# One decode step of attention and a gated feed-forward layer on one core: the V loads change their issuing engine

## The chip, the cores and the metric

The program runs on one core of one Trainium2 chip. The metric is the device time of one execution in microseconds (us); the number given for a kernel is the median of its runs. A profiled execution has its own time, and its trace covers a span that is a little shorter.

## What is computed

One token passes a pre-norm attention block whose keys and values lie in a cache, and then a feed-forward block with a ReLU gate. All is float32: 32 heads of 192 numbers each, 8192 cached positions, a model width of 640, and 1536 in the feed-forward block.

```python
h  = x + A(layernorm(x), k_cache, v_cache, wq, wo)
h2 = h + B(layernorm(h), W_gate, W_up, W_down)

def A(x, k_cache, v_cache, wq, wo):
    q = (x @ wq) as (B, H, 1, Dh)
    scores = einsum("bhqd,bhkd->bhqk", q, k_cache) * Dh ** -0.5
    o = einsum("bhqk,bhkd->bhqd", softmax(scores), v_cache)
    return o as (B, 1, H * Dh) @ wo

def B(x, W_gate, W_up, W_down):
    gate, up = x @ W_gate, x @ W_up
    return (where(gate > 0, gate, 0) * up) @ W_down
```

The caches are by far the largest inputs: 32 heads with 6.29 MB of K and 6.29 MB of V each, 403 MB of the 446 MB that are read.

## The kernel before

The 8192 positions of a head lie as 64 positions on each of 128 partitions, so one head's K, or its V, is one tile of 128 x 12288 numbers, loaded by one DMA of 128 rows of 49,152 bytes. All these tiles come from the pool `kv`, which has three places of that size and no more; the three loads of `wq` at the start and the feed-forward weights `ffn_a` and `ffn_b` at the end use the same three places. A load into a place waits until the readers of the tile that was there have finished.

In what follows K(h) and V(h) are the tiles of head h. Per head the work is this.

- **K to scores.** VectorE multiplies K by the query in four pieces (line 183), GpSimd adds the upper half of each product to the lower (line 184), and VectorE sums what is left in four pieces (line 188). After the last of these K's place is free.
- **Softmax.** The generator `softmax_steps` is run between the pieces of the next head's line 183: maximum over a partition (193), a transpose on TensorE (195), maximum over all (198), a broadcast on TensorE (200), the scaled maximum and the exponential on ScalarE (202, 205), the sum over partitions on TensorE (207) and its reciprocal on VectorE (210). So the softmax of head h lies in head h+1's scores.
- **Values.** 32 matmuls on TensorE (line 225, which the profile counts as 64) read all of V(h) and the weights `p`; after the last of them V's place is free. ScalarE then scales the result into `ob` (line 228).
- **Output.** `finish_steps` transposes `ob` on TensorE and VectorE (240, 244), also between the pieces of a later head, and once per group of four heads (two groups of two at the end) multiplies by that group's part of `wo` (254), 1.97 MB for four heads, loaded into a pool of its own with two places.

The query of a head (line 169) is a small matmul into one of two PSUM buffers.

The main loop asks in iteration h for K(h+1), then for V(h), then does the scores of head h+1 and the values of head h. All loads of the loop are issued by SP, on its one DMA queue, in the order K(1), V(0), K(2), V(1) and so on; only the two tiny loads of `x` are issued by ScalarE. A wait in front of a load holds up everything behind it on the issuing engine. A Tile scheduler turns the program into one instruction stream per engine and decides which of the three places each tile gets. The calls marked `keep` hold VectorE's order as written; the rest may be moved.

After the loop the tail loads `W_up` and part of `W_gate` into `ffn_a`, the rest of `W_gate` and `W_down` into `ffn_b`, 11.8 MB in all, each when a place is free (lines 294 to 298), and does the feed-forward block while the weights arrive.

Of the kernel before, what the change touches and what calls it, by code (L numbers as in the profile page):

```python
# [14 lines left out]
def kernel(  # L15
# [12 lines left out]
    nc = tc.nc  # L28
# [9 lines left out]
    TW = R * DH  # L38
# [11 lines left out]
    kf, vf = kc[0], vc[0]  # L50
# [20 lines left out]
    for j in range(0, DJ, 2):  # L71
        n = min(2, DJ - j)
# [1 line left out]
        nc.sync.dma_start(t3, wq_v[:, j:j + n, :])  # L74
        wq_ts += [t3[:, i, :] for i in range(n)]

    def load_kv(src, h, parts):
        t = kv.tile([P, 2 * TW], F32, name="kv_t")
        v = src[h].rearrange("(p r) d -> p (r d)", p=P)
        b = 0  # L80
        for n in parts:
            nc.sync.dma_start(t[:, b:b + n], v[:, b:b + n])  # L82
            b += n
        return t

    def load_wo(gi):
        hs = GROUPS[gi]
        j = len(hs) * DH // P
        t = wts.tile([P, j, D], F32, tag="wo_t", name="wo_t")
        r0 = hs[0] * DH  # L90
        nc.sync.dma_start(t, wo[r0:r0 + len(hs) * DH, :].rearrange("(p j) n -> p j n", p=P))
        return t
# [73 lines left out]
    def query(h):  # L166
        g, i = divmod(h, HPQ)
        q = ps_q.tile([P, QB], F32, tag="q", name="q")
        nc.tensor.matmul(q[:, 0:DH], sel[:, g, :], q4[:, i * DH:(i + 1) * DH], start=True, stop=True)  # L169
        return q[:, 0:DH]  # L170
# [5 lines left out]
    def head_step(q, kt, *works):  # L176


        sc = small.tile([P, NS], F32, name="sc")
        k3 = kt.rearrange("p (r d) -> p r d", d=DH)  # L180
        parts = [(i0, k3[:, i0:i0 + SUB, :]) for i0 in range(0, NS, SUB)]
        for i0, ks in parts:
            keep(nc.vector.tensor_mul(ks, ks, q[:, None, :].to_broadcast([P, SUB, DH])))  # L183
            nc.gpsimd.tensor_add(ks[:, :, 0:HD], ks[:, :, 0:HD], ks[:, :, HD:DH])  # L184
            for w in works:
                next(w, None)
        for i0, ks in parts:
            keep(nc.vector.reduce_sum(sc[:, i0:i0 + SUB], ks[:, :, 0:HD], axis=AX.X))  # L188
        return sc

    def softmax_steps(sc, res):
        mp = small.tile([P, 1], F32, name="mp")
        keep(nc.vector.reduce_max(mp, sc, axis=AX.X))  # L193
        pt = ps_s.tile([P, 512], F32, name="ps_small")
        keep(nc.tensor.transpose(pt[0:1, 0:P], mp, ident))  # L195
        yield
        m1 = small.tile([1, 1], F32, name="m1")
        keep(nc.vector.reduce_max(m1, pt[0:1, 0:P], axis=AX.X))  # L198
        pb = ps_s.tile([P, 512], F32, name="ps_small")
        nc.tensor.matmul(pb[:, 0:1], ones[0:1, :], m1, start=True, stop=True)  # L200
        nb = small.tile([P, 1], F32, name="nb")
        nc.scalar.mul(nb, pb[:, 0:1], -SCALE)  # L202
        p = small.tile([P, NS], F32, name="p")
        rs = small.tile([P, 1], F32, name="rs")
        nc.scalar.activation(p, sc, AF.Exp, bias=nb, scale=SCALE, accum_out=rs)  # L205
        pl = ps_s.tile([P, 512], F32, name="ps_small")
        nc.tensor.matmul(pl[:, 0:1], ones, rs, start=True, stop=True)  # L207
        yield
        rl = small.tile([P, 1], F32, name="rl")
        keep(nc.vector.reciprocal(rl, pl[:, 0:1]))  # L210
        res += [p, rl]
        yield
# [8 lines left out]
    def values_of(h, p, rl, vt):  # L221
        po = pos[h % 2]
        for i in range(NP):
            g = i % NQ
            nc.tensor.matmul(po[g * Q:g * Q + 2, :], p[:, 2 * i:2 * i + 2],  # L225
                             vt[:, 2 * i * DH:(2 * i + 2) * DH], start=(i < NQ), stop=(i >= NP - NQ))
        ob = small.tile([P, 2 * DH], F32, name="ob")
        nc.scalar.activation(ob, po, AF.Copy, scale=rl)  # L228
        return ob

    def finish_steps(h, ob, oT, wo_t):

        gi, i = group_of[h]
        U = NQ // len(GROUPS[gi])
        W = DH // U
        pt = ps_s.tile([P, 512], F32, name="ps_small")
        for u in range(U):
            q0 = (i * U + u) * Q
            for k in range(2):
                nc.tensor.matmul(pt[q0:q0 + Q, 0:W], par[:, k, :], ob[:, k * DH + u * W:k * DH + (u + 1) * W],  # L240
                                 start=(k == 0), stop=(k == 1))
        yield
        s = slice(i * U * Q, (i + 1) * U * Q)
        keep(nc.vector.transpose(oT[s], pt[s, 0:W].rearrange("p (c j) -> p j c", c=Q)))  # L244
        yield
        split = h >= H - 2
        if not split and i < len(GROUPS[gi]) - 1:
            return
        if not split:
            s = slice(0, P)  # L250
        J = wo_t.shape[1]
        for j in range(J):
            for g in range(NQ):
                nc.tensor.matmul(acc[g * Q:(g + 1) * Q, :], oT[s, j, :], wo_t[s, j, g * DG:(g + 1) * DG],  # L254
                                 start=False, stop=(h == H - 1 and j == J - 1))
        yield

    sc = head_step(query(0), load_kv(kf, 0, [2 * TW]))
    done = iter(())
    for h in range(H):  # L260
        gi, i = group_of[h]
        if i == 0:
            wo_t = load_wo(gi)
            oT = small.tile([P, len(GROUPS[gi]) * DH // P, Q], F32, tag="oT", name="oT")
        sm = []
        soft = softmax_steps(sc, sm)
        if h + 1 < H:
            kt = load_kv(kf, h + 1, [2 * TW])
            vt = load_kv(vf, h, [2 * TW])
            sc = head_step(query(h + 1), kt, soft, done)  # L270
        else:
            vt = load_kv(vf, h, [TW] + [TW // 4] * 4)
        for w in (soft, done):
            for _ in w:
                pass
        done = finish_steps(h, values_of(h, *sm, vt), oT, wo_t)
# [99 lines left out]
```

## Time and profile before

| | |
|---|---|
| median of 3 runs | 1045.99 us (1045.82 to 1046.0) |
| the profiled execution | 1045.67 us, of which the trace spans 1043.9 us |
| VectorE busy | 666.0 us, 64% of the span |
| GpSimd busy | 440.1 us, 42% |
| TensorE busy | 409.2 us, 39% |
| ScalarE busy | 45.5 us, 4% |
| read from HBM | 445.91 MB, 427 GB/s over the span |

All traces here are of one core. Times in rows are in us from the start of the span unless marked ns. A row of a timeline has the start, the length, the engine, the line, the operation, output and input, the count, and in brackets the idle time of the engine before it and what ended that. SPq and ACTq are the DMA-issuing instructions of SyncE and ScalarE. A row of the windows has the stretch, busy time and count of instructions for TensorE, its weight loads, VectorE, ScalarE and GpSimd, then the TensorE clock granted, the busy share of the 16 DMA engines, and GB/s.

### The profile page before, as it was taken

How to read it: one execution, taken by the hardware profiler on the slowest of the kernel's cores; microseconds unless marked ns; L12 is line 12 of the kernel's file. 1: busy time of each engine (PE TensorE's matmuls, PEld its weight loads, DVE VectorE, ACT ScalarE, POOL GpSimd, SP SyncE). 2: the span in 40 equal slices, each digit the busy share in tenths (PEclk: the TensorE clock that was granted, in tenths of full speed). 3: DMA queues.
4: the chain of work that ended last, by engine and by line, in shares of the span. 5: the costliest groups of instructions: out<-in, count | busy, mean ns of one | idle time of the engine just before them, and what ended most of it. 6: DMA issues, size and time to landing. Idle time of an engine off the chain costs nothing.

```text
span 1043.9 us, 7403 instructions
## 1 busy us (share of the span) xinstructions
PE 409.2 (39%) x3136; PEld 151.0 (14%) x3136; DVE 666.0 (64%) x418; ACT 45.5 (4%) x140; POOL 440.1 (42%) x139
## 2 busy tenths in 40 slices
PE   1603443343345333343432443343233444432475
PEld 0101111111112111121111111121111211111122
DVE  1086777566667766467775666677664667766551
ACT  0000000000000000000000000000000000000010
POOL 0055555344455544245553444455542455544330
PEclk9856665666666566666666666665566666656678
DMA  9999999999999999999999999999999999999997
GB/s 392 445 433 428 424 444 426 435 426 443 426 432 428 439 430 422 438 432 433 428 437 430 435 428 436 429 434 428 433 424 443 430 433 434 428 432 428 435 419 302
DMA packets 13003, 446.39 MB, mean 428 GB/s; under 512 B 1573, under 2 KB 1577, under 8 KB 3114
## 3 DMA queue, kind: packets, MB, share of 16 engines
q1 hardware_dynamic: 12824, 445.92, 99.2%
q8 instruction: 24, 0.39, 0.2%
q14 instruction: 9, 0.07, 0.0%
q10 hardware_dynamic: 146, 0.01, 0.0%
HBM read 445.91 MB, written 0.00 MB: 427 GB/s over the span
## 4 chain that ended last, share of the span: by engine, by line
DMA 62%; DVE 24%; PE 10%; issue 3%; SPq 0%; ACTq 0%; ACT 0%; DVEq 0%
DMA kv_t<-in_A_k_cache_dram 57%; DVE kv_t L183 19%; PE po L225 8%; DVE sc L188 3%; DMA xrow<-in_A_x_dram 2%; DMA ffn_b<-in_B_W_down_dram 2%; DMA ffn_a<-in_B_W_up_dram 2%; PE q L169 1%; PE qp L160 1%; DVE oT L244 1%; DVE m L198 0%; DVE rl L210 0%; DVE mp L193 0%; SPq L82 0%; PE acc L150 0%
## 5 line engine op out<-in xcount | busy, mean ns | idle before, releaser
L184 POOL TENSOR_TENSOR kv_t<-kv_t 128x1536 f32<-128x1536 f32 x128 | 438.2, 3445 | 559.6 <-DVE mp L193 247.4
L183 DVE TENSOR_TENSOR kv_t<-kv_t,q 128x3072 f32<-128x3072 f32 x128 | 427.4, 3342 | 321.1 <-DMA kv_t<-in_A_k_cache_dram 311.5
L225 PE MATMUL po<-kv_t,p 128*2 128x384 f32 x2048 | 224.4, 601 | 9.7 <-DMA kv_t<-in_A_v_cache_dram 9.7
L188 DVE TENSOR_REDUCE sc<-kv_t 128x16 f32<-128x1536 f32 x128 | 215.0, 1739 | 0.0
L195 PE MATMUL ps_small<-ident,mp 128*1 128x128 f32 x32 | 11.8, 368 | 367.6 <-DVE mp L193 367.6
L169 PE MATMUL q<-q,sel 128*128 128x192 f32 x64 | 29.6, 565 | 148.9 <-DVE kv_t L183 148.9
L225 PEld LDWEIGHTS po<-kv_t,p 128*2 128x2 f32 x2048 | 54.7, 97 | 168.9 <-issue 154.3
L195 PEld LDWEIGHTS ps_small<-ident,mp 128*1 128x1 f32 x32 | 2.5, 79 | 389.6 <-issue 355.5
L240 PE MATMUL ps_small<-ob,par 128*32 128x192 f32 (+1 forms) x144 | 44.5, 479 | 0.7 <-ACT ob L228 0.7
L200 PE MATMUL ps_small<-m,ones 1*128 1x1 f32 x64 | 18.4, 354 | 51.9 <-DVE m L198 51.9
L169 PEld LDWEIGHTS q<-q,sel 128*128 128x128 f32 x64 | 14.9, 289 | 156.1 <-DVE kv_t L183 107.5
L228 ACT ACTIVATE ob<-po,rl 128x384 f32<-128x384 f32 x32 | 18.6, 580 | 432.3 <-PE po L225 432.3
L254 PE MATMUL acc<-wo_t,oT 128*32 128x160 f32 (+1 forms) x408 | 33.5, 452 | 0.4 <-DVE oT L244 0.4
L202 ACT ACTIVATE nb<-ps_small 128x1 f32<-128x1 f32 x32 | 5.5, 171 | 495.6 <-PE ps_small L200 495.6
L200 PEld LDWEIGHTS ps_small<-m,ones 1*128 1x128 f32 x64 | 15.7, 303 | 71.8 <-DVE m L198 71.8
L207 PE MATMUL ps_small<-rs,ones 128*128 128x1 f32 x64 | 18.6, 359 | 18.9 <-ACT p L205 18.9
L254 PEld LDWEIGHTS acc<-wo_t,oT 128*32 128x32 f32 (+1 forms) x408 | 18.7, 157 | 6.9 <-DVE oT L244 1.3
L160 PE MATMUL qp<-kv_t,xn 128*32 128x512 f32 x120 | 17.4, 736 | 5.3 <-DMA kv_t<-in_A_wq_dram 4.3
L207 PEld LDWEIGHTS ps_small<-rs,ones 128*128 128x128 f32 x64 | 15.8, 308 | 24.9 <-ACT p L205 24.9
L240 PEld LDWEIGHTS ps_small<-ob,par 128*32 128x32 f32 x144 | 16.7, 153 | 16.9 <-issue 7.5
L244 DVE STREAM_TRANSPOSE oT<-ps_small 32x192 f32<-32x192 f32 (+1 forms) x32 | 11.7, 364 | 10.4 <-PE ps_small L240 9.8
L205 ACT ACTIVATE p<-sc,nb 128x64 f32<-128x64 f32 x32 | 11.1, 348 | 1.0
(72 smaller groups left out, 73.4 us busy)
## 6 DMA issues: line engine op xcount, KB each, us to landing
kv_t<-in_A_k_cache_dram SPq DMA_DIRECT2D x32, 6144.0 KB, 37.0
kv_t<-in_A_v_cache_dram SPq DMA_DIRECT2D x31, 6144.0 KB, 23.1
wo_t<-in_A_wo_dram SPq DMA_DIRECT2D x7, 1920.0 KB, 27.0
kv_t<-in_A_wq_dram SPq DMA_DIRECT2D x2, 6144.0 KB, 17.8
ffn_a<-in_B_W_up_dram SPq DMA_DIRECT2D x1, 3840.0 KB
kv_t<-in_A_wq_dram SPq DMA_DIRECT2D x1, 3072.0 KB, 39.6
kv_t<-in_A_v_cache_dram SPq DMA_DIRECT2D x1, 3072.0 KB, 31.0
kv_t<-in_A_v_cache_dram SPq DMA_DIRECT2D x4, 768.0 KB, 34.6
```

The source lines that it names most:

```text
L160: nc.tensor.matmul(qps[b][g * Q:(g + 1) * Q, :], xn[:, j:j + 1].to_broadcast([P, Q]), wq_ts[j][:, c0:c0 + QB], start=(j == 0), stop=(j == ...
L169: nc.tensor.matmul(q[:, 0:DH], sel[:, g, :], q4[:, i * DH:(i + 1) * DH], start=True, stop=True)
L183: keep(nc.vector.tensor_mul(ks, ks, q[:, None, :].to_broadcast([P, SUB, DH])))
L184: nc.gpsimd.tensor_add(ks[:, :, 0:HD], ks[:, :, 0:HD], ks[:, :, HD:DH])
L188: keep(nc.vector.reduce_sum(sc[:, i0:i0 + SUB], ks[:, :, 0:HD], axis=AX.X))
L200: nc.tensor.matmul(pb[:, 0:1], ones[0:1, :], m1, start=True, stop=True)
L207: nc.tensor.matmul(pl[:, 0:1], ones, rs, start=True, stop=True)
L225: nc.tensor.matmul(po[g * Q:g * Q + 2, :], p[:, 2 * i:2 * i + 2], vt[:, 2 * i * DH:(2 * i + 2) * DH], start=(i < NQ), stop=(i >= NP - NQ))
L228: nc.scalar.activation(ob, po, AF.Copy, scale=rl)
L240: nc.tensor.matmul(pt[q0:q0 + Q, 0:W], par[:, k, :], ob[:, k * DH + u * W:k * DH + (u + 1) * W], start=(k == 0), stop=(k == 1))
L244: keep(nc.vector.transpose(oT[s], pt[s, 0:W].rearrange("p (c j) -> p j c", c=Q)))
L254: nc.tensor.matmul(acc[g * Q:(g + 1) * Q, :], oT[s, j, :], wo_t[s, j, g * DG:(g + 1) * DG], start=False, stop=(h == H - 1 and j == J - 1))
```

## The change

`load_kv` gets a parameter for the issuing engine, and the loop passes ScalarE for V. So V(0) to V(30) are issued by ScalarE on its own DMA queue. K, `wo`, the five parts of V(31) and the feed-forward weights stay with SP.

```diff
-    def load_kv(src, h, parts):
+    def load_kv(src, h, parts, eng=nc.sync):
         t = kv.tile([P, 2 * TW], F32, name="kv_t")
         v = src[h].rearrange("(p r) d -> p (r d)", p=P)
         b = 0
         for n in parts:
-            nc.sync.dma_start(t[:, b:b + n], v[:, b:b + n])
+            eng.dma_start(t[:, b:b + n], v[:, b:b + n])
             b += n
         return t
...
         if h + 1 < H:
             kt = load_kv(kf, h + 1, [2 * TW])
-            vt = load_kv(vf, h, [2 * TW])
+            vt = load_kv(vf, h, [2 * TW], nc.scalar)
             sc = head_step(query(h + 1), kt, soft, done)
         else:
             vt = load_kv(vf, h, [TW] + [TW // 4] * 4)
```

The diff does not show what it does to the order and to the three places. On SP, early in the loop, the stream stands as follows before; 310, 384 and 458 are K(2), K(3) and K(4), and 312, 386 and 460 are V(1), V(2) and V(3). The brackets name the semaphores waited for: DVE_49 counts VectorE's work, PE_49 TensorE's, DMAHW ones the landing of earlier loads.

```order
L82 DMA kv_t_310<-in_A_k_cache_dram 128x12288 [waits DMAHW5_49,DVE_49]
L82 DMA kv_t_312<-in_A_v_cache_dram 128x12288 [waits DMAHW7_49,DMAHW2_49,DVE_49]
L82 DMA kv_t_384<-in_A_k_cache_dram 128x12288 [waits DMAHW0_49,PE_49]
L82 DMA kv_t_386<-in_A_v_cache_dram 128x12288 [waits DMAHW1_49,DVE_49]
L82 DMA kv_t_458<-in_A_k_cache_dram 128x12288 [waits DMAHW2_49,PE_49]
L82 DMA kv_t_460<-in_A_v_cache_dram 128x12288 [waits DMAHW6_49,DMAHW3_49,DVE_49]
```

From K(3) on a K waits for TensorE, that is for the value matmuls of the V three loads back, and a V waits for VectorE, that is for the scores of its own head: the three places go round. The same place of the changed kernel's SP stream, where 535 and 633 are K(5) and K(6):

```order
L82 DMA kv_t_310<-in_A_k_cache_dram 128x12288 [waits DMAHW5_49,DVE_49]
L91 DMA wo_t_532<-in_A_wo_dram 128x3840
L82 DMA kv_t_384<-in_A_k_cache_dram 128x12288 [waits DMAHW7_49,DMAHW4_49,DVE_49]
L82 DMA kv_t_458<-in_A_k_cache_dram 128x12288 [waits DMAHW6_49,DMAHW1_49,DVE_49]
L82 DMA kv_t_535<-in_A_k_cache_dram 128x12288 [waits DMAHW4_49,DMAHW0_49,DVE_49]
L82 DMA kv_t_633<-in_A_k_cache_dram 128x12288 [waits DMAHW6_49,DMAHW2_49,DVE_49]
```

Every K now waits for VectorE: the scheduler gives K(h) the place of K(h-2), so two of the three places are K's and the third is V's alone. On ScalarE, in the same part of the program, where 242 and 312 are V(0) and V(1), the changed kernel has:

```order
L82 DMA kv_t_242<-in_A_v_cache_dram 128x12288 [waits DMAHW4_49,DMAHW0_49]
L202 ACTIVATE nb_259<-ps_small_257 128x1 [waits PE_49]
L205 ACT_TABLE_LOAD [waits DVE_49]
L205 ACTIVATE p_261,rs_262<-sc_224,nb_259 128x64 [waits Activation_49]
L228 ACTIVATE ob_308<-po0_216,rl_268 128x384 [waits DVE_49,PE_49]
L82 DMA kv_t_312<-in_A_v_cache_dram 128x12288 [waits DMAHW2_49,DMAHW0_49]
```

V(1) stands behind `ob` of head 0, which waits for the value matmuls of head 0. No wait of its own for TensorE is needed in front of V(1), since ScalarE has passed that point. On TensorE the pieces of one head, before (`-`) and now (`+`):

```order
 L207 MATMUL ps_small<-rs,ones 128x1
-L169 MATMUL q<-q_212,sel 128x192
-L225 MATMUL po_216<-kv_t,p 2x384 x32
+L225 MATMUL po_216<-kv_t,p 2x384 x32
+L169 MATMUL q<-q_212,sel 128x192
 L195 MATMUL ps_small<-ident,mp 1x128
 L240 MATMUL ps_small<-ob,par 32x192 x2
```

The query matmul, which waits for a PSUM buffer that line 183 reads, has moved from in front of the value matmuls to behind them; the next head's transpose of the maxima (195) stands behind the value matmuls in both. VectorE's order is the same.

At the end of SP's stream, 2738 is V(31), and the changed kernel has:

```order
L82 DMA kv_t_2650<-in_A_k_cache_dram 128x12288 [waits DMAHW6_49,DMAHW3_49,DVE_49]
L82 DMA kv_t_2738<-in_A_v_cache_dram 128x6144 [waits DMAHW5_49,DMAHW0_49,DVE_49]
L82 DMA kv_t_2738<-in_A_v_cache_dram 128x1536
L82 DMA kv_t_2738<-in_A_v_cache_dram 128x1536 [waits DMAHW7_49]
L294 DMA ffn_a_2833<-in_B_W_up_dram 128x7680 [waits DMAHW4_49,DMAHW2_49,PE_49]
L295 DMA ffn_a_2833<-in_B_W_gate_dram 128x4608 [waits DMAHW3_49]
L296 DMA ffn_b_2834<-in_B_W_gate_dram 128x3072 [waits DVE_49]
```

V(31) takes K(30)'s place, `ffn_a` now takes V(30)'s and waits for TensorE's value matmuls of head 30, and `ffn_b` takes K(31)'s. Before, `ffn_a` waited for VectorE (K(31)'s scores) and `ffn_b` for TensorE.

## The prediction

> **What bounds the kernel now.** I read the 40 slices of the span first, then the chain that ended last, then who waits for whom.
>
> ```profile
> DMA  9999999999999999999999999999999999999997
> GB/s 392 445 433 428 424 444 426 435 426 443 426 432 428 439 430 422 438 432 433 428 437 430 435 428 436 429 434 428 433 424 443 430 433 434 428 432 428 435 419 302
> q1 hardware_dynamic: 12824, 445.92, 99.2%
> DMA 62%; DVE 24%; PE 10%; issue 3%; SPq 0%; ACTq 0%; ACT 0%; DVEq 0%
> SPq L82 <- DVE sc L188: 638.6, 31, 20.8
> ```
>
> The 16 DMA engines are busy in every slice but the last, at 422 to 445 GB/s, and one queue (q1, SP's) carries nearly everything. No compute engine is near its limit. The kernel is bound by the bytes, and only idle time of the DMA engines costs anything. SP itself waits 638.6 us for line 188, and yet the engines stay full, since what SP has issued is deep enough. One head shows how deep:
>
> ```profile
> 489.15 0.33 SPq L82 DMA_DIRECT2D kv_t<-in_A_v_cache_dram  x1
> 490.14 0.33 SPq L82 DMA_DIRECT2D kv_t<-in_A_k_cache_dram  x1
> 497.76 3.35 DVE L183 TENSOR_TENSOR kv_t<-kv_t,q 128x3072 f32<-128x3072 f32 x1 [8.64 <-DMA kv_t<-in_A_k_cache_dram]
> 505.58 0.35 ACT L205 ACTIVATE p<-sc,nb 128x64 f32<-128x64 f32 x1
> 511.72 6.73 DVE L188 TENSOR_REDUCE sc<-kv_t 128x16 f32<-128x1536 f32 x4
> 512.79 7.25 PE L225 MATMUL po<-kv_t,p 128*2 128x384 f32 x64
> 518.47 0.33 SPq L82 DMA_DIRECT2D kv_t<-in_A_v_cache_dram  x1
> 520.11 0.33 SPq L82 DMA_DIRECT2D kv_t<-in_A_k_cache_dram  x1
> 520.12 0.58 ACT L228 ACTIVATE ob<-po,rl 128x384 f32<-128x384 f32 x1 [14.11 <-PE po L225]
> 526.75 3.35 DVE L183 TENSOR_TENSOR kv_t<-kv_t,q 128x3072 f32<-128x3072 f32 x1 [8.31 <-DMA kv_t<-in_A_k_cache_dram]
> 520.11 40.28 DMA kv_t<-in_A_k_cache_dram
> ```
>
> A K lands at 497.7 and the next at 526.7, and between them one V and one K went over: 29.0 us, so **one tile alone takes 14.5 us** (6.29 MB at 434 GB/s). When the V of 518.47 is issued, the K issued at 490.14 still needs 8 us, and the next K is issued 1.6 us later. The last row, from the chain, is a head with a `wo` load in it: landing at 560.4, 33.7 us after 526.7, so `wo` costs about 4.6 us.
>
> **What the change does to this loop.** It makes nothing smaller: the same bytes pass through the same 16 engines, and SP's 31 issues of 0.33 us were behind waits. It changes when a load is issued. By the order rows, V(h+1) stands on ScalarE behind `ob` of head h, and it has one place of its own. Let E be the end of the value matmuls of head h. Before, V(h+1) was issued at 518.47, ahead of that E (520.04) and behind a K in flight. Now no V is in ScalarE's queue from the landing of V(h) until shortly after E. That gap must be filled by K.
>
> The cost of the gap needs four durations.
>
> ```profile
> 0.75 1.34 SPq L74 DMA_DIRECT2D kv_t<-in_A_wq_dram  x3
> 1.75:2.00 0.25, 0.00 (x0) 0.00 (x0) 0.13 (x1) 0.23 (x1) 0.20 (x2) 1.00 5.99 1769
> 1041.12 0.65 SPq L348 DMA_DIRECT2D out_dram<-o  x1
> 1042.25:1042.50 0.25, 0.00 (x0) 0.00 (x0) 0.00 (x0) 0.00 (x0) 0.00 (x0) 0.70 0.04 10
> 1039.50:1039.75 0.25, 0.25 (x12) 0.04 (x4) 0.00 (x0) 0.00 (x0) 0.00 (x0) 1.00 0.03 10
> 1040.17 0.48 PE L344 MATMUL pd<-ffn_b,guT 128*32 128x160 f32 x8 [0.30 <-DMA ffn_b<-in_B_W_down_dram]
> 966.08 7.59 PE L225 MATMUL po<-kv_t,p 128*2 128x384 f32 x64 [5.68 <-DMA kv_t<-in_A_v_cache_dram]
> ```
>
> From issue to the first bytes it takes 1.0 us (0.75 to 1.75) and 1.1 us (1041.12 to 1042.25): I take 1.1. From the last bytes (about 1039.6) to the first matmul that reads them: 0.6. The 64 matmuls take 7.25 us above, and 7.6 where TensorE had idled 5.68 us first; it will idle longer now, so 7.6. `ob` adds 0.6. So V's queue is empty for 0.6 + 7.6 + 0.6 + 1.1 = **9.9 us per head**.
>
> When does K come? K(h+4) follows the last sum over K(h+2). The softmax of h+1 lies in K(h+2)'s scores, and its transpose (195) is behind the value matmuls of h on TensorE, so VectorE, which runs ahead now, is held there until E. The steps from there, in the head at 497.76:
>
> ```profile
> 501.39 0.37 PE L195 MATMUL ps_small<-ident,mp 128*1 128x128 f32 x1 [11.33 <-DVE mp L193]
> 501.69 1.49 PE L240 MATMUL ps_small<-ob,par 128*32 128x192 f32 x4
> 504.73 0.38 DVE L244 STREAM_TRANSPOSE oT<-ps_small 32x192 f32<-32x192 f32 x1
> 505.12 3.35 DVE L183 TENSOR_TENSOR kv_t<-kv_t,q 128x3072 f32<-128x3072 f32 x1
> 508.39 0.16 DVE L210 RECIPROCAL rl<-ps_small 128x1 f32<-128x1 f32 x1
> 508.47 3.33 DVE L183 TENSOR_TENSOR kv_t<-kv_t,q 128x3072 f32<-128x3072 f32 x1
> 511.86 1.00 PE L169 MATMUL q<-q,sel 128*128 128x192 f32 x2 [5.20 <-DVE kv_t L183]
> ```
>
> After E come the query (1.0, now behind the matmuls), 195 (0.4), 240 (1.5), 244 (0.4), two pieces of 183 with 210 between (3.35, 0.1, 3.33) and line 188 (6.7): 16.9. With 1.1 more, **K(h+4) has its first bytes at E+18.0**. The moved query costs nothing else: it is for a head three ahead, and it takes a 5 us wait out of the way of the value matmuls.
>
> How two queues share the engines this trace shows once, at the start:
>
> ```profile
> 0.74 0.41 ACTq L65 DMA_DIRECT2D xT<-in_A_x_dram  x1
> 18.77 0.16 DVE L127 TENSOR_REDUCE s<-xT 128x1 f32<-128x5 f32 x1 [16.89 <-DMA xT<-in_A_x_dram]
> DMA to landing us min/median/max: 17.8/28.7/39.6
> ```
>
> 128 rows of 20 bytes on ScalarE's queue took 18 us, to 18.7, beside the first `wq` tile of 128 rows of 49,152 bytes, which was issued at 0.75 and landed after 17.8 us (the last row, of the three `wq` loads), at 18.55. The tiny rows finished with the big ones, so the queues went row by row. K and V rows are equally long, so each gets **half while both are there**. The Trainium skill, "DMA: Bandwidth & Descriptors", section "Queues, rings and completion order", has each engine go round its queues packet by packet; the `xT` row agrees.
>
> Now one cycle, with E = 0 and K's queue just empty. V alone from 1.7 to 16.2; its matmuls end at 24.4. K starts at 18.0: **idle 1.8**. K alone to 26.1, where the next V starts: 8.1 done, 6.4 left, at half speed until 38.9, V having 6.4. The next K starts at 24.4 + 18.0 = 42.4; V alone has 9.9 by then, and the last 4.6 take 9.2, to 51.6. Its E is 59.8, the next V starts at 61.5. K has 4.6 at 51.6 and needs 9.9 more: done at 61.5. K's queue is empty as V starts, so the cycle closes. **Two heads take 59.8 us for 58.0 of transfer**; on every second head the engines idle 1.8.
>
> - *Loop:* two cycles per four heads idle 3.6. One `wo` load (4.6, behind a K on SP) falls in these and fills one idle at best: 1.8 to 3.6 per four heads, or 12.6 to 25 over 28 heads. `wo` is longer than an idle, so I take **+16**, nearer the low end.
> - *Start:* V(0) is issued behind the last copy of line 164, at 46.4, and from 47.5 shares with K(0), which had some 8 us to go (the rows below). Its scores begin about 8 us later; K(1) and K(2) keep the engines full meanwhile, and the second `wo` load, which SP now issues right behind K(2), covers the gap before V(1). 0 to 2; **+0.7**.
>
> ```profile
> 45.83 0.58 ACT L164 COPY q<-qp 128x512 f32<-128x512 f32 x1 [1.12 <-PE qp L160]
> 55.95 13.15 DVE L183 TENSOR_TENSOR kv_t<-kv_t,q 128x3072 f32<-128x3072 f32 x4 [31.51 <-DMA kv_t<-in_A_k_cache_dram]
> ```
>
> - *End:* `ffn_a` now waits for the value matmuls of head 30, and all of V(31) is issued once K(30) is summed, so lands before V(30) is through. Nothing is queued between V(30)'s landing and the first bytes of `ffn_a`: 0.6 + 7.6 + 1.1 = **+9.3**. Before, that cover was there:
>
> ```profile
> 971.86 4.11 SPq L82 DMA_DIRECT2D kv_t<-in_A_v_cache_dram  x6
> 982.91 3.35 DVE L183 TENSOR_TENSOR kv_t<-kv_t,q 128x3072 f32<-128x3072 f32 x1 [11.07 <-DMA kv_t<-in_A_k_cache_dram]
> 1003.54 0.33 SPq L294 DMA_DIRECT2D ffn_a<-in_B_W_up_dram  x1
> ```
>
>   V(30) and V(31) were queued from 971.86, 29 us of transfer behind a K that landed at 982.9, so to about 1012, and `ffn_a` joined them at 1003.54. The 11.8 MB of the tail take 27 us then as now.
> - *Not seen before:* the rate with both queues loaded, and how unevenly the 16 engines finish. The slices differ by 422 to 445, so I bound the first at ±3% over the 22 us per cycle that are shared, ±0.7 a cycle, ±10 in all, and take 0, the mean of equal rows. A tile alone ends with its slowest engine, and at the very end the engines fell idle over some 5 us, from 70% busy to 3%, 2.5 in the mean:
>
> ```profile
> 1034.00:1036.00 2.00, 1.40 (x36) 0.97 (x32) 0.00 (x0) 0.00 (x0) 0.00 (x0) 0.88 0.70 285
> ```
>
>   Once per cycle that is 0 to 35; I take 0, as in the slices, since K's rows mostly run behind a V.
>
> Sum: +26.0 on 1045.67 of the profiled execution, 1071.7; the median stands 0.3 above that execution, so **1072**.
>
> **Rivals.** (a) *The loop has no idle, only the tail costs.* K's start at E+18.0 is a sum of small terms against V's end at E+16.2; 1.8 us less, and the loop is full: 1045.99 + 9.3 = 1055. For it: `wo` and uneven engines smear the ends. Against it: each term has its own row. Chance 0.15.
>
> (b) *ScalarE's queue gets less than half.* With 40% the same cycle gives V's end at 53.9 and K done at 61.5, E at 62.1 and the next V at 63.8: idle 1.8 + 2.3 = 4.1 per cycle, 57 over 14 cycles, less up to 13 for `wo`, plus 10: 1100 to 1113. For it: `xT` landed after `wq`, not before. Against: by 0.2 us. Chance 0.14.
>
> (c) *Two queues fill the engines better, and it is faster.* It decides in the 22 us per cycle in which both are loaded: to win back 26 us over 14 cycles, 1.86 each, the rate there must rise by 8%, from 434 to 470 GB/s; at 10% it wins 31 and gives 1041. Against it: engines at 99.2%, no slice over 445. Chance 0.11, of which 0.05 falls within the measurement's reach of no change. Beside it stands a page: the Trainium skill, same page, section "Issuing engines are not separate DMA queues", says that issuing from several engines saves only the issuing time; by that alone the time would stay at 1046, since that time is hidden. No run here shows it yet.
>
> **How the numbers follow.** The forecast, equal halves and the 1.8 us idle, has 0.60 and by its bounds taken one at a time (12.6 to 25, 0 to 2, ±10, 0 to 35) 1062 to 1107. The range 1050 to 1108 takes in (a) and about half of (b), and leaves out (c) and smaller shares for V, 0.18 together. About 0.2%, 2 us, is what a measurement can tell from no change: faster 0.06, within it 0.05, slower 0.89.
>
> **What would show it.** In the trace after: ScalarE's V issue right behind each `ob`; landings of V alternately some 16 and 26 us after their issue; periods of value matmuls alternating near 24 and 35; VectorE waiting at line 198 for TensorE; DMA share below 9 tenths in the last slices, with a gap of 9 us before `ffn_a`. If V's landings take 30 us or more, (b) holds; if GB/s rises above 445 while both queues run, (c); if the tail's gap alone is there, (a). A K that arrives late, so that VectorE waits for DMA and not for TensorE, would refute my cycle.

## The result and the profile after

| | before | after |
|---|---|---|
| median of 4 runs | 1045.93 us (1045.82 to 1046.0) | 1091.54 us (1088.74 to 1094.69) |
| ratio | | 1.0437, 95% interval 1.0408 to 1.0466 |
| the profiled execution | 1045.67 us, span 1043.9 | 1092.02 us, span 1090.1 |

The change costs 45.6 us, 4.4%. The direction was as forecast, the size was not: 1072 was predicted, and 1091.5 lies in the upper half of the range.

The page of the changed kernel, the rows that answer to those of before: the busy share of the DMA engines and their rate by slice, the two queues, and the chain that ended last by engine.

```profile
DMA  9999999999999989999999999999999999999957
GB/s 399 432 436 408 423 433 387 424 426 435 376 433 402 436 361 399 431 397 433 402 410 397 423 435 392 432 432 433 412 413 426 424 435 392 433 426 430 407 227 328
q1 hardware_dynamic: 8360, 250.88, 54.0%
q10 hardware_dynamic: 4610, 195.04, 42.3%
DMA 73%; PE 22%; DVE 3%; another core or an unknown queue 1%; issue 0%; ACT 0%; ACTq 0%; DVEq 0%
```

The digits hardly show it. The second row does: slices of 361 to 408 GB/s stand among slices of 430 and more, where before all but the first and the last two had 422 to 445. The queues' shares add up to 96.3% where before one had 99.2%; that is an average, and it hides that the slow stretches are short. In the chain VectorE has fallen from 24% to 3%, and TensorE has risen from 10% to 22%, by the pages nearly all of it in the value matmuls (8% before, 21% now). So I read who waits for whom:

```profile
PE po L225 <- DMA kv_t<-in_A_v_cache_dram: 616.1, 30, 29.1
DVE m L198 <- PE ps_small L195: 293.4, 29, 16.4
DVE kv_t L183 <- DMA kv_t<-in_A_k_cache_dram: 60.3, 6, 38.5
SPq L82 <- DVE sc L188: 763.1, 31, 37.7
```

TensorE waits for V in every head, and VectorE waits for TensorE at line 198 (29 times, 10.1 us each) rather than for K (six times). K loads wait for VectorE. The chain, in order of time, shows the V's of four heads from issue to landing, and the timeline what lies between:

```profile
533.21 17.74 DMA kv_t<-in_A_v_cache_dram
557.94 29.94 DMA kv_t<-in_A_v_cache_dram
595.17 21.49 DMA kv_t<-in_A_v_cache_dram
624.92 25.59 DMA kv_t<-in_A_v_cache_dram
```

```profile
533.15 0.58 ACT L228 ACTIVATE ob<-po,rl 128x384 f32<-128x384 f32 x1 [34.48 <-PE po L225]
533.21 0.33 ACTq L82 DMA_DIRECT2D kv_t<-in_A_v_cache_dram  x1
533.74 0.28 DVE L198 TENSOR_REDUCE m<-ps_small 1x1 f32<-1x128 f32 x1 [15.79 <-PE ps_small L195]
535.06 3.35 DVE L183 TENSOR_TENSOR kv_t<-kv_t,q 128x3072 f32<-128x3072 f32 x1
541.66 6.72 DVE L188 TENSOR_REDUCE sc<-kv_t 128x16 f32<-128x1536 f32 x4
548.41 25.07 SPq L82 DMA_DIRECT2D kv_t<-in_A_k_cache_dram  x2
550.99 6.81 PE L225 MATMUL po<-kv_t,p 128*2 128x384 f32 x64 [14.95 <-DMA kv_t<-in_A_v_cache_dram]
```

This is the predicted cycle: V is issued right behind `ob`, VectorE is released at the same moment, runs two pieces of line 183 and four of line 188, and the next K is issued (548.41; the row covers two K issues, the second behind a wait). But K came in time: E was 533.1, so its issue was at E + 15.3 instead of the predicted E + 16.9, and its first bytes were under way before the last of V had landed at 550.95. The predicted 1.8 us between V's end and K's first bytes, in which nothing flows, is not there. The windows of this cycle (columns as in the section on the profile before) show what is there instead:

```profile
529.00:541.00 12.00, 6.23 (x55) 2.26 (x47) 6.59 (x5) 1.19 (x4) 2.50 (x1) 0.78 0.90 369
546.00:556.00 10.00, 5.01 (x44) 1.26 (x48) 9.04 (x5) 0.00 (x0) 4.22 (x2) 0.60 0.94 380
556.00:584.00 28.00, 3.96 (x35) 1.68 (x27) 20.73 (x12) 1.19 (x4) 14.82 (x5) 0.65 1.02 439
```

While both queues are loaded (556 to 584) the rate is 439 GB/s. From 529 to 541, where the K that was queued runs out and the next V begins, it is 369, and from 546 to 556, where V runs out and K begins, 380. Against 434 that is 12 x 65/434 = 1.8 us and 10 x 54/434 = 1.2 us lost, while the engines were idle all together for moments at most.

The end of the span, in the windows and, from the timeline, the issue of the first feed-forward load:

```profile
1044.00:1046.00 2.00, 0.00 (x0) 0.00 (x0) 0.00 (x0) 0.00 (x0) 0.00 (x0) 0.50 0.06 25
1046.00:1054.00 8.00, 7.42 (x60) 1.87 (x64) 0.00 (x0) 0.00 (x0) 0.00 (x0) 0.60 0.00 0
```

```profile
1054.83 0.33 SPq L294 DMA_DIRECT2D ffn_a<-in_B_W_up_dram  x1
```

V(30) has landed, its 64 matmuls run, and no byte flows until `ffn_a` is issued behind them.

To see where 46 us went I counted the trace's DMA packets. An engine is idle while none of its packets runs; the figures are means over the 16 engines, in us, and in brackets the time in which all were idle together. The loop goes here from 104 us to the last V issue on ScalarE (to 972 us where ScalarE issues none), the end from there. "Slow rows" are rows of K, V, `wq` or `W_up` that took over 0.45 us longer than the usual 1.815 us for 49,152 bytes (in proportion for shorter ones, 0.908 for 24,576), with their number and the sum of their excess over 16.

```
kernel                  span   start      loop           end          slow rows
before                 1043.9  2.1 (1.8)   0.0 (  0.0)   6.8 ( 4.1)    40   1.6
after                  1090.1  2.1 (1.8)  20.8 (  1.6)  18.0 (13.8)   292  15.0
e11_query_first        1094.6  2.2 (1.8)  26.1 (  2.2)  15.8 (12.4)   299  15.7
e2_one_queue           1044.2  2.1 (1.8)   0.1 (  0.0)   6.4 ( 4.1)    55   2.4
e3_tail_sp             1091.3  2.1 (1.8)  20.6 (  1.3)  17.5 (11.4)   305  15.7
e5_values_late         1096.1  2.1 (1.8)  19.2 (  2.7)  23.9 (19.7)   312  15.8
e6_halves              1135.0  2.1 (1.8)  63.8 ( 36.7)  13.4 ( 9.6)   354  17.7
e7_both_halves         1060.2  2.2 (1.8)   1.7 (  0.0)  12.6 ( 9.8)   104   5.1
e8_k_halves            1063.9  2.2 (1.8)   2.6 (  0.0)  16.9 (13.3)   122   6.3
e10_one_queue_halves   1048.6  2.0 (1.8)   0.0 (  0.0)   6.8 ( 4.0)    39   1.6
e4_ring_two_queues     1340.4  4.0 (2.6) 269.2 (221.8)  10.5 ( 7.5)   411  22.4
```

For the change: 20.8 in the loop, 11.2 more at the end, 13.4 more in slow rows, 45.4 of the 46.2 by which the span grew. In the loop all engines together were idle for only 1.6 us.

Each of the loop's idle stretches ends either with rows of V or with rows of K. Sorted by that (means over the engines, us):

```
kernel                  K has run out, V next    V has run out, K next
after                          16.8                      4.0
e11_query_first                21.5                      4.5
e6_halves                      57.0                      6.8
e7_both_halves                  0.9                      0.9
e8_k_halves                     0.6                      2.0
```

So four fifths of the loop's idle time in the changed kernel come not from a late K but from the other change of queues: the K that is queued runs out before the next V begins. The packets of V show why. From the last row of one V to the first row of the next it took 10.4 to 13.0 us from head 3 on, 11.4 in the mean, where the prediction had 9.9. From V's last row to the first matmul that reads it, 0.36 to 0.49 us passed on seven heads, where K had only just begun or was not there, and 2.2 to 2.6 us on thirteen, where K's rows had been running beside V's; the others lie between. The cycle above ends like this:

```profile
585.00:594.00 9.00, 6.08 (x56) 1.61 (x60) 0.00 (x0) 0.00 (x0) 0.49 (x1) 0.64 0.97 421
594.00:597.00 3.00, 2.81 (x25) 1.10 (x13) 0.66 (x2) 0.65 (x2) 0.00 (x0) 1.00 0.74 229
```

The last row of the V issued at 557.94 ended at 585.6, engines began to run out of K at 594.0, 8.4 us later, and the first row of the next V started at 596.2, 10.6 us later.

### The profile page after: what moved, and what is told of

Same layout as the page of the kernel before. It is cut to its first block, busy times and chain, and to the rows that moved or that the text cites. A ratio compares the mean times of both kernels' runs of the same rounds, so it can differ in the third digit from the quotient of the medians.

```text
span 1090.1 us, 7358 instructions
## 1 busy us (share of the span) xinstructions
PE 357.3 (33%) x3136; PEld 123.2 (11%) x3136; DVE 666.7 (61%) x418; ACT 45.6 (4%) x140; POOL 439.1 (40%) x139
## 4 chain that ended last, share of the span: by engine, by line
DMA 73%; PE 22%; DVE 3%; another core or an unknown queue 1%; issue 0%; ACT 0%; ACTq 0%; DVEq 0%
DMA kv_t<-in_A_v_cache_dram 66%; PE po L225 21%; DMA kv_t<-in_A_k_cache_dram 3%; DMA xrow<-in_A_x_dram 2%; DVE kv_t L183 2%; DMA ffn_b<-in_B_W_down_dram 2%; DMA ffn_a<-in_B_W_up_dram 1%; PE qp L160 1%; DVE sc L188 1%; ACT L205 0%; PE acc L150 0%; ACT ob L228 0%; PE ps_small L200 0%; PE ps_small L207 0%
## 5 line engine op out<-in xcount | busy, mean ns | idle before, releaser
L225 PE MATMUL po<-kv_t,p 128*2 128x384 f32 x2048 | 237.6, 631 | 616.1 <-DMA kv_t<-in_A_v_cache_dram 616.1
L198 DVE TENSOR_REDUCE m<-ps_small 1x1 f32<-1x128 f32 x32 | 8.9, 278 | 293.4 <-PE ps_small L195 293.4
L169 PE MATMUL q<-q,sel 128*128 128x192 f32 x64 | 19.1, 383 | 29.9 <-DVE kv_t L183 29.9
L240 PE MATMUL ps_small<-ob,par 128*32 128x192 f32 (+1 forms) x144 | 26.2, 320 | 3.4 <-ACT ob L228 1.2
L207 PE MATMUL ps_small<-rs,ones 128*128 128x1 f32 x64 | 12.9, 270 | 18.9 <-ACT p L205 18.9
L254 PE MATMUL acc<-wo_t,oT 128*32 128x160 f32 (+1 forms) x408 | 15.9, 301 | 1.7 <-DVE oT L244 1.6
L195 PE MATMUL ps_small<-ident,mp 128*1 128x128 f32 x32 | 8.9, 279 | 21.5 <-DVE mp L193 21.5
L200 PE MATMUL ps_small<-m,ones 1*128 1x1 f32 x64 | 12.5, 262 | 6.4 <-DVE m L198 6.4
L240 PEld LDWEIGHTS ps_small<-ob,par 128*32 128x32 f32 x144 | 11.4, 110 | 17.4 <-ACT ob L228 14.1
L207 PEld LDWEIGHTS ps_small<-rs,ones 128*128 128x128 f32 x64 | 10.1, 199 | 22.9 <-ACT p L205 20.9
L254 PEld LDWEIGHTS acc<-wo_t,oT 128*32 128x32 f32 (+1 forms) x408 | 12.2, 109 | 3.8 <-DVE oT L244 3.3
L200 PEld LDWEIGHTS ps_small<-m,ones 1*128 1x128 f32 x64 | 9.8, 190 | 16.2 <-DVE m L198 7.9
```

## The experiments

The theory at this point: V's own queue is empty for about ten microseconds between two heads, K is often just not there, or only just, and every time an engine runs dry it loses. Four kernels went first, e2, e3, e5 and e6; e11 is told where it belongs and was run last.

### One queue, with the places of the changed kernel

The three places become two pools, two places for K and one for V, as the scheduler had chosen in the changed kernel; only the issuing engine goes back. (The lines of this kernel stand one further down, line 226 for 225, and so do those of e5_values_late.)

```diff
-    kv = ctx.enter_context(tc.tile_pool(name="kv", bufs=3))
+    kv = ctx.enter_context(tc.tile_pool(name="kv", bufs=2))
+    vp = ctx.enter_context(tc.tile_pool(name="vp", bufs=1))
...
-            vt = load_kv(vf, h, [2 * TW], nc.scalar)
+            vt = load_kv(vf, h, [2 * TW], nc.sync, vp)
```

> All loads go back to SP's one queue, but the places stay as in the changed kernel (two for K, one for V), so V(h+1) still waits for the value matmuls of head h. Theory (an empty V queue costs only where no K is queued; on one queue the next K stands behind each V and covers the 9.9 us): 1046 to 1050 us, DMA share 9 in every slice but the last. Rival (the single place of V, or its late issue, is what costs): 1075 us or more, with slices below 9. The gap in front of ffn_a is covered too by the theory, since V(31) is queued behind V(30).

Measured: 1046.2 us, ratio to before 1.0005 (0.9996 to 1.0014). The page's share of the DMA engines and its queue, and from the timeline the value matmuls of one head with SP's issues behind them:

```profile
DMA  9999999999999999999999999999999999999997
q1 hardware_dynamic: 12824, 445.92, 99.3%
```

```profile
513.38 6.49 PE L226 MATMUL po<-kv_t,p 128*2 128x384 f32 x64
519.93 0.33 SPq L83 DMA_DIRECT2D kv_t<-in_A_v_cache_dram  x1
520.85 0.37 SPq L83 DMA_DIRECT2D kv_t<-in_A_k_cache_dram  x1
```

V(h+1) is issued right at the end of the value matmuls of head h, as late as in the changed kernel, and it costs nothing, since the K behind it on the same queue keeps the engines busy through the next gap. So neither V's late issue nor its single place is what costs. One order moved back with it: the query matmul (170 here) stands ahead of the value matmuls again, as in the kernel before. So a kernel with that alone followed.

### The query's place put back, V on ScalarE

The query of head h+2 is emitted ahead of the value matmuls of head h, and both are kept in that order; all else is the changed kernel.

```diff
+    qn = query(1)
...
-            sc = head_step(query(h + 1), kt, soft, done)
+            sc = head_step(qn, kt, soft, done)
+            if h + 2 < H:
+                qn = query(h + 2)
```

> The kernel with all loads on one queue also has the query matmul (line 169) in front of the value matmuls again, as before; the changed kernel has it behind them. This kernel is the changed kernel with only that put back: V stays on ScalarE, places and all other orders are the same. Theory (the second queue is what costs): TensorE comes to the transpose behind the value matmuls up to 1.0 us sooner, so K is issued at most 1.0 us sooner after E; the uneven ends in the loop shrink by at most that on every second head, 14 us, and the end stays: 1077 to 1092 us. Rival (the query's place is what costs): 1060 us or less. A value above 1095 would mean that the query in front of the value matmuls holds them up itself.

Measured: 1095.36 us, ratio 1.0462 (1.0435 to 1.0488), not told apart from the changed kernel's by the intervals. The rival is out: the query's place is not what costs, the second queue is. The range was missed as well, since the gain that I had allowed for did not come: the next K is issued 15.3 us behind E in the mean, in this kernel as in the changed one, and the loop's idle time is 26.1 us, not less than 20.8. So this kernel does not test what a sooner K would be worth. The median lies 0.4 us above the 1095 named for a query that holds up the value matmuls; that is not what the trace shows, where the value matmuls still wait for V (30 times, 608.5 us).

### The last three V's back on SP

```diff
-            vt = load_kv(vf, h, [2 * TW], nc.scalar)
+            vt = load_kv(vf, h, [2 * TW], nc.scalar if h < 28 else nc.sync)
```

> V(0) to V(27) stay on ScalarE, V(28) to V(30) go back to SP; the last heads' places go round as before, and ffn_a waits for VectorE again. Theory (the end of the changed kernel loses 11 us because nothing is queued between V(30)'s landing and ffn_a, the rest is lost in the loop): 1092 - 11 = 1081 us, between 1076 and 1084, and no slice below 9 but the last. Rival (the loss at the end is only moved there and comes back elsewhere): 1088 us or more. Rival (the end is nearly all of the loss): 1055 us or less.

Measured: 1091.68 us, ratio 1.0434 (1.0411 to 1.0456). The expectation failed; the first rival came in. The gap at the end did go: idle time behind 1027 us fell from 18.0 to 6.0, about that of the kernel before (6.8). It came back at the handover. SP's issues there, from the timeline, and the windows around them:

```profile
965.37 0.33 SPq L82 DMA_DIRECT2D kv_t<-in_A_v_cache_dram  x1
965.80 0.37 SPq L82 DMA_DIRECT2D kv_t<-in_A_k_cache_dram  x1
```

```profile
950.00:960.00 10.00, 1.80 (x12) 0.40 (x16) 10.00 (x6) 0.00 (x0) 3.54 (x2) 0.50 0.42 182
960.00:970.00 10.00, 9.60 (x115) 4.16 (x107) 3.78 (x4) 1.19 (x4) 4.04 (x2) 0.91 0.44 159
```

V(28) stands ahead of K(30) on SP and waits for the value matmuls of head 27 until 965.3. K(30) has been free to go since its place was summed at 953.8 (948.70 + 5.06, line 188) and waits behind it. Two windows at 0.42 and 0.44 lose 11.4 us, nearly all of the 12.0 that the end had gained.

### Value matmuls written behind the next softmax

V stays on ScalarE with the two pools; the value matmuls of head h are emitted, and kept, behind the softmax matmuls of head h+1, and `ffn_b` is queued ahead of `ffn_a`. (The diff leaves out the pools, the matmuls that are kept in order, and V's load, which is now written behind the value matmuls of the head before.)

```diff
-        done = finish_steps(h, values_of(h, *sm, vt), oT, wo_t)
+        if late:
+            done = late()
...
+        late = lambda h=h, sm=sm, vt=vt, oT=oT, wo_t=wo_t: finish_steps(h, values_of(h, *sm, vt), oT, wo_t)
```

> V stays on ScalarE, places two for K and one for V, but the value matmuls of head h are written behind the softmax steps of head h+1, so that TensorE does the transposes of line 195 first and VectorE is not held up by the value matmuls; ffn_b is queued before ffn_a. V's queue is still empty between two heads. Theory (K comes late because VectorE is held until E): VectorE's wait at the reduction over the transposed maxima goes from 293 us to under 40, the loop's idle of about 21 us goes, the slow first rows on an empty queue stay (some 10 to 14 us), and the end is mostly covered: 1055 to 1065 us. Rival (two loaded queues lose rate whatever the order): 1075 us or more, with no idle engines. Rival (the slow first rows cost nothing by themselves): 1046 to 1052.

Measured: 1102.82 us, ratio 1.0549 (1.051 to 1.0589): a miss for the theory as it was written. The kernel did not do what it was made for, as its costliest groups show (busy and mean ns, then the idle time before them):

```profile
L199 DVE TENSOR_REDUCE m<-ps_small 1x1 f32<-1x128 f32 x32 | 8.9, 278 | 281.8 <-PE ps_small L196 281.8
```

VectorE still waits 281.8 us at the reduction: the transpose of head h+2 now stands behind the value matmuls of head h, so the hold moved by one head. The loop lost as much as before (19.2), and the end 5.9 us more, with `ffn_a` last. The step "VectorE is held until E" was therefore not tested. A kernel without that hold would need another order of the output steps too (line 244 also waits for E); it was not tried.

### V in halves

```diff
-            vt = load_kv(vf, h, [2 * TW], nc.scalar)
+            vt = load_kv(vf, h, [TW, TW], nc.scalar)
```

> Each V of ScalarE is loaded by two DMAs of half a tile (128 rows of 24,576 bytes), so half of the value matmuls run before the second half has landed and V's queue is empty for 0.6 + 3.8 + 0.6 + 1.1 = 6.1 us a head instead of 9.9; places and orders are those of the changed kernel. Theory: the loop's idle of about 21 us falls to 8 or less, the end loses 3.8 us less: 1065 to 1078 us. Rival (what costs is not the length of V's gap but the sharing of two queues): 1087 us or more.

Measured: 1137.33 us. Its four times lie between 1115.84 and 1139.03, so no ratio is given for it; its trace is of an execution of 1136.97 us. Even the lowest is far from the 1065 to 1078 expected, and 24 us above the changed kernel: with V in halves the kernel became slower. The chain of waits has V alternating like this:

```profile
483.19 38.27 DMA kv_t<-in_A_v_cache_dram
526.79 18.39 DMA kv_t<-in_A_v_cache_dram
550.19 38.34 DMA kv_t<-in_A_v_cache_dram
```

On every second head V needs 38 us. At half the rate it would need 29. That number gave the missing piece: if the engines take the two queues in turn **row by row**, V's rows of 24,576 bytes against K's of 49,152 get one third, 14.5 x 3 = 43.5 us as long as K is there throughout. The share would then be set by the sizes of the rows. K, with two thirds, would be used up sooner, and a later V makes VectorE and the next K late too, so both queues are dry before the next V begins. Of this trace's idle time in the loop 57.0 us lie there, and all engines are idle together for 36.7 us.

### The rows the other way round, and equal

If that is so, halving K's rows helps as much as halving V's hurt, and halving both gives equal shares again.

```diff
-            kt = load_kv(kf, h + 1, [2 * TW])
+            kt = load_kv(kf, h + 1, [TW, TW])
```

> Only K is loaded in two DMAs of half a tile (rows of 24,576 bytes), V in whole rows of 49,152 bytes on ScalarE. Theory (shares go by the size of a row): V gets two thirds while both queues are loaded and lands 20 to 24 us after its issue on all heads instead of 18 and 30 in turn; every head takes the same time, K is there to fill V's gap, and some 10 us at the end and a few us of restarts remain: 1053 to 1066 us. Rival (shares go by bytes, or the loss comes from the gap in V's queue whatever the share): no change against the changed kernel, 1085 us or more.

> K and V are both loaded in two DMAs of half a tile each (rows of 24,576 bytes on both queues), otherwise the changed kernel. In e6_halves only V's rows were halved, and V landed 38 us after its issue on every second head, as if it had a third of the bytes while K was there. Theory (the engines take the queues in turn row by row, so the size of a row sets the share): equal rows give equal shares again, and the value matmuls start with the first half, so V's queue is empty for 6.1 us a head instead of 9.9; V lands 21 to 28 us after its issue on all heads, and the time is 1048 to 1065 us. Rival (halved V loads cost by themselves, through more DMAs or waits on ScalarE): 1110 us or more, as in e6_halves.

> e2_one_queue (all loads on SP, places as in the changed kernel) with K and V in two DMAs of half a tile each: the control for what halving costs by itself. Theory: nothing that can be measured, 1044 to 1050 us. Rival (rows of 24,576 bytes or the added DMAs are slower by themselves): 1060 us or more.

Measured: K halved 1061.84 us, ratio 1.0152 (1.0135 to 1.0169); both halved 1061.46 us, 1.0177 (1.0115 to 1.0239; one of its four times is 1074.92); both halved on one queue 1050.61 us, 1.0045 (1.003 to 1.006). Each lies in or beside its range (the last 0.6 above it), and both rivals of the two-queue kernels, at 1085 and 1110, are out. The V's of three heads in the chain with K halved:

```profile
482.26 25.66 DMA kv_t<-in_A_v_cache_dram
515.84 18.52 DMA kv_t<-in_A_v_cache_dram
542.70 25.66 DMA kv_t<-in_A_v_cache_dram
```

The alternation is weaker than 18 and 30, but it is not gone: over the run V took 18.5 to 26.5 us, where I had expected 20 to 24 throughout. With both halved the landings missed their 21 to 28 us too; from issue to V's last row it took 18 to 32 from head 3 on. In stretches in which nothing landed and both queues moved bytes, ScalarE's queue had 0.49 of the engine time in the changed kernel (273 us of such stretches), 0.31 with V's rows halved (209 us) and 0.61 with K's rows halved (143 us), by the packets of the trace; row by row gives 0.50, 0.33 and 0.67. The values depend on where such a stretch is taken to begin and end: counted only while V's rows were queued on all engines and K's rows ran beside them, they come out near 0.50, 0.35 and 0.73. The `wo` loads, whose rows have 15,360 bytes, are a check on their own: beside them V's whole rows had 0.76 of the engine time in the changed kernel and V's halved rows 0.60 in e6_halves, where row by row gives 0.76 and 0.62.

With K halved the loop's idle time is 2.6 us instead of 20.8 and the slow rows cost 6.3 instead of 15.0. What is left is mostly the end (16.9). The same two queues and the same places thus lose hardly anything in the loop once V gets the larger share: V's gap is no shorter (11.8 us in the mean), but 0.6 us are left of the 16.8 that were lost where K had run out. K was issued as late as before behind E (531.04, E + 15.3, in the cycle of the second row). The kernel with both halved, with no such share, loses as little; its V gap is 9.3 us. So a larger share is one way and a shorter gap beside equal rows another. What the two have in common is K's halved rows, beside which V's last row was 1.4 us ahead of its matmuls in the median with K halved, instead of 2.2; no run separates that from the share.

The halved rows themselves cost 4.4 us on one queue with the same places (1050.61 against 1046.2), so their loop gain is a little larger than the totals show.

### The places going round, with two queues

Three pools of one place each, taken in turn by all the tiles, force the places of the kernel before; V stays on ScalarE.

```diff
-    kv = ctx.enter_context(tc.tile_pool(name="kv", bufs=3))
+    rings = [ctx.enter_context(tc.tile_pool(name=f"kv{i}", bufs=1)) for i in range(3)]
...
-        t = kv.tile([P, 2 * TW], F32, name="kv_t")
+        t = kv_tile(name="kv_t")
```

> V on ScalarE as in the changed kernel, but the three places are forced to go round as in the kernel before, so K(h) waits for the value matmuls of the V three loads back, not for its own predecessor's scores. Theory (what decides is what is still queued when V's queue is empty): K(h+2) and V(h) are now both released by the same value matmuls, both queues are empty together for about 9.9 us on every head, and both transfers share to the end: about 9.9 + 29 = 38.5 us a head, 1285 us, DMA share near 0.75 through the loop. Rival (the places don't matter, the use of two queues does): about 1092 us, like the changed kernel.

Measured: 1342.14 us, one run. The chain with the V's of two heads, the page's DMA issues (count, KB each, median us to landing), and a window of one gap:

```profile
509.81 32.04 DMA kv_t<-in_A_v_cache_dram
548.85 31.94 DMA kv_t<-in_A_v_cache_dram
```

```profile
kv_t<-in_A_k_cache_dram SPq DMA_DIRECT2D x32, 6144.0 KB, 32.1
kv_t<-in_A_v_cache_dram ACTq DMA_DIRECT2D x31, 6144.0 KB, 32.1
```

```profile
501.00:510.00 9.00, 8.52 (x66) 2.23 (x67) 6.74 (x3) 0.27 (x1) 5.05 (x2) 0.65 0.00 1
```

K and V are issued together after each gap and both land after 32.1 us: equal rows, equal halves. In the gap nothing flows for nine microseconds. The mechanism of the prediction, unmixed, gives the loss that it should, and 57 us more than the 1285 expected. Part of that has a row: 1.1 + 29.0 + 0.6 = 30.7 us were expected from issue to matmuls, and 32.0 were measured, so a start from empty costs some 1.3 us beyond the gap.

No experiment beat the kernel before; the nearest, all loads on one queue, equals it.

## Why the prediction was right, and where it was short

- *The bound.* Right: only idle time of the DMA engines counts. All loads on one queue give 1046.2 whichever way V's issue waits.
- *What the change does.* Right: V behind `ob`, one place of its own, VectorE held at 198 by 195 behind the value matmuls (293 us), V's landings uneven (17.7 and 29.9 us in the rows above, 16 and 26 expected; later in the run less regular, 21.5 and 25.6). "K comes late and VectorE waits for DMA", which would have refuted it, is not in the trace: six waits in all.
- *Equal halves.* Right for equal rows (32.1 and 32.1 us), for the reason given: the queues take turns by rows, and V and K have equal rows. The Trainium skill, "DMA: Bandwidth & Descriptors", section "Queues, rings and completion order", has the engines alternate packet by packet. The kernels with halved rows (38 us against 18 to 26) agree with an alternation; but where that section has some 9 to 17 descriptors in a typical packet, one row is the turn here: in the trace before, the rows of `xT` start singly between rows of `wq`, sixteen in each 1.8 us over all engines.
- *Rate with two queues, taken 0.* Right: 439 GB/s where both are loaded, and rows of 49,152 bytes take 1.82 us in the median in both kernels.
- *Loop, +16.* **This is the step that fell short.** Its reason was a full stop of 1.8 us on every second head, between V's end and K's first bytes. K came 1.6 us earlier than I had added up: line 183 began 1.9 us after E, where query, 195, 240 and 244 had been summed one behind the other to 3.3. So there is no full stop there, and at that change of queues the whole loop has only 4.0 us of idle engines. What the loop lost instead lies mostly where the prediction had no loss, in "K's queue is empty as V starts, so the cycle closes": that cycle leaves K exactly the 9.9 us that V's gap lasts, with no margin. In the runs the gap was 11.4 us in the mean and K lasted less, 8.4 against 10.6 us in the cycle above. The term behind it is the 0.6 us from the last bytes to the first matmul, taken for every V; it was 2.2 to 2.6 us after a V that had shared the engines with K to its end. That the landing waits about one row of K there is a reading of these numbers (1.8 us more beside rows of 1.8 us, 0.9 more beside K's halved rows of 0.9 us), not shown by itself.
- *How unevenly the 16 engines finish, 0 to 35, taken 0.* The 20.8 us of idle engines in the loop are of this kind and lie within the bound. The reason given for the 0, "K's rows mostly run behind a V", was wrong: each queue gave out engine by engine before the other's rows came. The 13.4 us of slow first rows had no term in the sum. Together that is 34.2 against +16.
- *Luck.* That the time lies in the range owes much to the range's width: the +16 stood for stops that did not come, and the 35 that held the loss was reckoned for uneven ends alone.
- *End, +9.3.* Right in kind; 11.2 measured, with 8.2 us for the matmuls of head 30 (7.6 taken).
- *Start, +0.7.* Nothing: 2.1 us before and after.
- *Rivals.* (a), only the end costs, is out: 34 of the 46 us are in the loop. (b), less than half for ScalarE, is out by 32.1 and 32.1, though its time was near: in its cycle too K runs out before the next V, by 2.3 us. Two of V's landings, 30.2 and 31.9 us, passed the 30 set as its sign; V's rows start 3.3 to 3.8 us after the issue where K's fill the engines, instead of 1.1, and land late as above, which that sign had not allowed for. (c), that two queues fill better, is out. The page beside it, in the Trainium skill's "DMA: Bandwidth & Descriptors", section "Issuing engines are not separate DMA queues", would have left 1046; the kernels with V on SP and on ScalarE, places and waits the same, 1046.2 and 1091.5 (1095.4 with the query's place the same too), disagree with that.

The prediction's 422 to 445 GB/s for every slice but the last leaves out the first (392) and the last but one (419); nothing hangs on that. What is not shown by a run of its own is the split of the 34 us between idle engines and slow first rows: both come and go together in every kernel of the table.

## What to carry to other kernels

On one queue a load behind another covers a gap in its neighbour's stream for nothing; two streams that each wait for their own consumer can both be short at once, and the engines run dry one by one long before a slice of the profile shows it. Before splitting loads over queues, ask for each stream when its next load is issued, against when the last bytes of the other are gone, and ask it at both changes, from the first stream to the second and back. A sum that closes with no margin is no cover: here one queue gave out two microseconds before the other began on many heads, and by the reading above a late landing was enough for that. Where two queues must share, the sizes of their rows set the shares. Giving the larger rows to the stream that the critical chain waits for took most of the loop's loss away here, and so did halving the rows of both.

## What the runs showed of the hardware

- A row of 49,152 bytes takes 1.815 us when it follows another on its engine. The first sixteen rows of a queue that starts while the other queue is idle took 2.2 to 2.7 us in the mean in the changed kernel, and rows of 24,576 bytes 1.5 to 1.9 us instead of 0.91 in e6_halves: 0.4 to 1 us more at either size. Where the other queue was running on all 16 engines, the first rows took 1.815 to 1.85 us. It is the engine's start from idle that costs, not the queue's.
- Halving the rows from 49,152 to 24,576 bytes on one queue cost 4.4 us in 1046 (1050.61 against 1046.2 with the same places), where I had expected nothing.
- The two queues alternate by rows: about 0.3, 0.5 and 0.6 to 0.7 of the engine time for row sizes of 1:2, 1:1 and 2:1.
- A load whose last rows ran beside those of another queue was followed by its first matmul 2.2 to 2.6 us after its last row, and 0.36 to 0.49 us where it had had the engines to itself. Its first row started 1.0 us after the issue where the other queue had run out, and mostly 3.3 to 3.8 us where that queue filled the engines.
